# A chunked recurrence feeding routed experts: the block product moves behind u, and the fourth chunk of each group takes over work of the fifth

## Chip, cores and metric

The kernel runs on one core of a Trainium2 chip. Its engines are TensorE (PE; PEld are its weight loads), VectorE (DVE), ScalarE (ACT), GpSimd (POOL) and the queue of SyncE (SP). Each engine takes its own instructions in program order; semaphores tie them together. The metric is the device time of one execution in microseconds (us).

## What is computed

Three stages follow one another: a recurrence over 768 tokens for 4 x 8 heads of width 40, a routed layer of eight experts (320 to 1024 to 320), and a dense layer (320 to 2048 to 320, squared ReLU) on 3,072 tokens. Only the recurrence matters here:

```python
for t in range(S):
    y[:, :, t] = np.einsum('bhd,bhde->bhe', rt, state)
    Sa = np.einsum('bhde,bhe->bhd', state, at)
    state_decay = state * wt[:, :, None, :] - np.einsum('bhd,bhe->bhde', Sa, bt)
    state = state_decay + np.einsum('bhd,bhe->bhde', vt, kt)
```

The output of the recurrence chooses each token's expert (the largest of eight logits), and the tokens are scattered to their experts' slots in memory.

## The kernel before

**Chunks.** The recurrence runs over 24 chunks of 32 tokens, for all 32 heads at once. Within a chunk the dependence of tokens on each other is a triangular system: its inverse is built once per chunk, ahead of time, and the state then passes from chunk to chunk by matrix products. m is c % 4.

**The steps of chunk c**, with the tile that each writes (the letters in the traces' rows):

- `u`: new values, 64 small matmuls into pu from lu and ru, then four ScalarE copies into vu. lu is one buffer.
- `state`: 64 matmuls into ps; `state_decay`: two VectorE products into ru, which `u` of the next chunk reads. `state_t`: 16 transposes into pn, two copies into rhsY.
- `vu_t`: 16 transposes into pv, two copies into vut; `scores`: 32 matmuls into pq; `scores_mask`: two VectorE products into rq.
- `y`: 64 matmuls into py; `gate_in`: one VectorE product into xt (the chunk's output). It reads rhsY, of which there are two (c % 2), so it stands ahead of `nat_k(c + 2)`, which writes the same one.
- `nat_k`: keys, eight transposes into pk, two ScalarE copies into rhsY. `nat_n`, `nat_a`, `nat_pc`: the left side X of the block product and Pn, by transposes pa and ScalarE copies.
- `block_T`: four ScalarE copies of a chunk's inverse from TT into TB (two of them, c % 2). `solve`: the block product, 16 matmuls px from X and TB and two copies into lu.
- `load`: the chunk's E in four DMAs on ScalarE's queue. `scan`: four VectorE instructions (two scans, Pc, a reciprocal). `scale`: three products on GpSimd. `gram`: 64 matmuls into G; `gram_mask`: a ScalarE copy GM and a VectorE product N.

E is loaded nine chunks ahead, scanned and scaled nine (or eight) ahead, and its Gram products are made LA = 7 ahead.

**The inverse.** One inverse serves a group of four chunks: `inv_start` transposes GM into L and lists 27 products; each character "v" that `inv` is given makes the next one on VectorE, as a product (pr) and a reduction (into Tt or Xm). The 27th is followed by a transpose from Tt into TT. PLAN and FIRST say how many products each of the four chunks makes. A group's inverse is made during the group ahead of it.

**The gate.** `gate.xT`, `gate.logits`: transposes gpt and matmuls pl with ScalarE copies; `choose`: eight tiny VectorE instructions; `count`: eight matmuls pc, an exponential and a copy; `rank`, `rank_batch`: tiny instructions, on GpSimd until chunk 16 (`eng=G`), on VectorE after; `scatter`: a DMA issued by GpSimd. Batches are chosen and counted around every fourth chunk.

**Order.** The whole order is written out by hand (`manual_schedule`). Chunks 1 to 19 go through `chunk(c)`; chunk 0 and those from 20 on have an order of their own in `run`. PSUM tiles come from three rotating large buffers (`big`) and two small ones (`small`): the next tile in a buffer waits until the last one has been read.

Of the kernel before, what the change touches and what calls it, by code (L numbers as in the profile page):

```python
# [13 lines left out]
ALU = mybir.AluOpType  # L14
AX = mybir.AxisListType
# [20 lines left out]
class Attention:  # L36
# [478 lines left out]

    def run(self, extra, weights):
        LA, SHIFT = 7, 20
        PLAN, FIRST = (11, 9, 5, 2), (11, 9, 5, 2)
        V, G = self.nc.vector, self.nc.gpsimd
        gate = self.gate  # L520

        def fill(c, i):
            if 1 <= c <= 2:
                extra(5 * c + i, 5 * c + i + 1)
            elif 5 <= c < 14 and i == 2:
                extra(10 + c, 11 + c if c < 13 else None)

        def wload(i):
            r = (self.L, self.Tt)[i % 2].rearrange("p a b -> p (a b)")
            weights.load(i, r[:, 0:704], 1)  # L530
# [57 lines left out]
        def chunk(c):  # L588

            m, bt = c % 4, gate.batch(c)  # L590
            plan = FIRST if c < 4 else PLAN
            early, nxt = bt if c < 17 else None, gate.batch(c + 1) if c < 16 else None
            self.u(c)
            if bt and 17 <= c:
                gate.choose(*bt)
            self.y(c - 1)
            self.nat_k(c + 1)
            self.load_r(c + 1)
            self.load(c + LA + 2, 3)
            fill(c, 0)  # L600
            self.gram(c + LA)
            self.gram_mask(c + LA, True)
            if m != 3:
                self.block_T(c + 1)
            self.state(c)
            self.state_decay(c)
            self.vu_t(c)
            if m == 3:
                self.block_T(c + 1)
            self.load(c + LA + 2, 0)  # L610
            fill(c, 1)
            self.gate_in(c - 1)
            if m == 3 or c == 1:
                self.scan(c + LA + 1)
                self.scale(c + LA + 1)
            self.scores(c)
            self.scores_mask(c)
            if m == 0:
                self.inv_start(c // 4 + 1, lambda k, h: G)
                gate.invert()  # L620
            self.solve(c + 1)
            if early:
                gate.count(*early)
            self.load_v(c + 2)
            self.store_x(c - 1)
            self.load_w(c + LA + 4)
            self.load(c + LA + 2, 1)
            fill(c, 2)
            gate.xT(c - 1)
            if bt and 17 <= c:  # L630
                gate.count(*bt)
            self.nat_n(c + 2)
            self.nat_a(c + 2)
            self.nat_pc(c + 2)
            self.state_t(c + 1)
            self.load(c + LA + 2, 2)
            fill(c, 3)
            gate.logits(c - 1)
            if m != 3:
                self.inv("v" * plan[m])  # L640
            if nxt:
                gate.choose(*nxt)
            if m == 2:
                self.inv("v" * plan[3])
            if bt:
                gate.rank(*bt, eng=G if early else None)
                gate.rank_batch(*bt, eng=G if early else None)
            gate.scatter(1)
            if m != 2:
                self.scan(c + LA + 2)  # L650
                self.scale(c + LA + 2)
            fill(c, 4)
            if c == 19:
                wload(0)
                wload(1)
# [5 lines left out]
        for c in range(NC - 1):  # L661
            if 1 <= c < SHIFT:
                chunk(c)
                continue
            m = c % 4
# [64 lines left out]
            self.nat_a(c + 2)  # L730
            self.nat_pc(c + 2)
            if c == 0:
                self.inv("v" * FIRST[0])
            if c >= 21:
                self.gate_in(c, x22 if c == 22 else None)
# [20 lines left out]
        c = NC - 1  # L756
# [43 lines left out]
class Gate:  # L800
# [76 lines left out]
    def choose(self, c0, c1):  # L877
        V = self.nc.vector
        k = c1 - c0
        L = self.lg[:, c0:c1]  # L880

        def t(shape, nm):
            return self.wp.tile(shape, F32, tag=nm + str(k), name=f"{nm}_{c0}", bufs=2 if k == 1 and nm == "ex" else 1)

        def bc(z):
            return z.unsqueeze(2).to_broadcast([128, k, 8])

        mx, d, ex, eq, m2 = t([128, k], "mx"), t([128, k, 8], "d"), t([128, k, 8], "ex"), t([128, k, 8], "eq"), t([128, k], "m2")
        self.ex[c0] = ex
        V.tensor_reduce(mx, L, axis=AX.X, op=ALU.max)  # L890
        V.tensor_tensor(d, L, bc(mx), ALU.subtract)
        self.d[c0] = d
        V.tensor_scalar(eq, d, 0.0, None, ALU.is_equal)
        V.tensor_tensor(eq, eq, self.we.unsqueeze(1).to_broadcast([128, k, 8]), ALU.mult)
        V.tensor_reduce(m2, eq, axis=AX.X, op=ALU.max)
        V.tensor_tensor(self.oh[:, c0:c1], eq, bc(m2), ALU.is_equal)
        V.tensor_tensor(eq, self.oh[:, c0:c1], self.ie.unsqueeze(1).to_broadcast([128, k, 8]), ALU.mult)
        V.tensor_reduce(self.ei[:, c0:c1], eq, axis=AX.X, op=ALU.add)

    def count(self, c0, c1):  # L900

# [9 lines left out]
    def ahead(self, c0, c1, i, car, r, V):  # L911

        k = c1 - c0
        pr = self.pr[c0]
        ab, q = (self.wp.tile([128, k, 8], F32, tag=f"{nm}{i}{k}", name=f"{nm}{i}_{c0}") for nm in ("ab", "rq"))
        V.tensor_copy(ab[:, 0], car)
        for j in range(1, k):
            V.tensor_tensor(ab[:, j], ab[:, j - 1], pr[:, 2 * i + 1, j - 1], ALU.add)
        V.tensor_tensor(car, ab[:, k - 1], pr[:, 2 * i + 1, k - 1], ALU.add)
        V.tensor_tensor(ab, ab, pr[:, 2 * i], ALU.add)  # L920
        V.tensor_tensor(q, ab, self.oh[:, c0:c1], ALU.mult)
        self.sum8(V, r, q)

    def sum8(self, eng, out, q):

        if eng is self.nc.vector:
            eng.tensor_reduce(out, q, axis=AX.X, op=ALU.add)
            return
        eng.tensor_tensor(q[:, :, 0:4], q[:, :, 0:4], q[:, :, 4:8], ALU.add)
        eng.tensor_tensor(q[:, :, 0:2], q[:, :, 0:2], q[:, :, 2:4], ALU.add)  # L930
        eng.tensor_tensor(out, q[:, :, 0], q[:, :, 1], ALU.add)

    def invert(self):

# [25 lines left out]
    def rank_batch(self, c0, c1, eng=None):  # L960
        V, k = eng or self.nc.vector, c1 - c0
        sm = self.wp.tile([128, k], F32, tag=f"sm{k}", name=f"sm_{c0}")
        self.ahead(c0, c1, 1, self.cntb, self.lp[:, c0:c1], V)
        self.sum8(V, sm, self.ex.pop(c0))
        V.tensor_scalar_add(sm, sm, 1e-9)
        self.sums.append((c0, c1, sm))
        if eng is None:
            self.invert()
# [732 lines left out]
```

## Time and profile before

| | |
|---|---|
| median of 3 runs | 1104.91 us (1104.29 to 1106.89) |
| profiled execution | 1107.82 us, span of its trace 1106.0 us |
| busy, share of the span | PE 85%, PEld 76%, DVE 68%, ACT 51%, POOL 28% |
| granted TensorE clock, mean | 0.909 |
| DMA | 122.71 MB, mean 111 GB/s |
| start of `u` of chunks 1, 4, 8, 12, 16, 20 | 88.32, 144.93, 213.76, 283.02, 352.12, 415.14 us |

The span reaches from the first to the last instruction of one profiled execution. A row of the timeline gives start, length, engine, line, operation, tile written and tiles read, shapes (partitions x elements), and in brackets the idle time of the engine before it with what ended it; rows of one kind are merged. "issue" is idle time for which the trace shows no cause. PEclk is the granted clock as a share of 2.4 GHz.

### The profile page before, as it was taken

What the parts mean: (1) busy time and instruction counts of PE and PEld (TensorE: products, weight loads), DVE (VectorE), ACT (ScalarE), POOL (GpSimd) and SP (SyncE); (2) the same over time, 40 slices, a digit from 0 to 9 for tenths busy, and PEclk for the clock granted to TensorE, in tenths of its full rate; (3) what the DMA queues carried; (4) which work ended last, traced back from release to release, by engine and by line L of the source; (5) the groups of instructions that cost most, each with busy time, mean ns of one, the idle gap of its engine ahead of it and who ended that gap; (6) DMA issues with size and microseconds to landing.
All of it is one profiled execution on the core that took longest, in us unless ns stands there. A gap on an engine that the chain in (4) does not pass through costs nothing.

```text
span 1106.0 us, 30639 instructions
## 1 busy us (share of the span) xinstructions
PE 937.6 (85%) x12526; PEld 843.9 (76%) x12526; DVE 757.0 (68%) x1515; ACT 568.1 (51%) x1302; POOL 304.8 (28%) x432
## 2 busy tenths in 40 slices
PE   5257677777887878899899998799999999999995
PEld 3147676766776767768889998789899999999995
DVE  7999979799696784566887878867544444444432
ACT  7135575565665657635456655556534343434432
POOL 5523162341633110114555555414301010000000
PEclk7567889697897988889999999999999999999998
DMA  7735644364551324146766766434100000000000
GB/s 189 197 99 166 195 135 143 113 181 124 157 137 47 94 69 125 41 133 178 231 221 205 218 217 203 143 101 124 48 24 25 25 25 24 1 25 1 23 2 27
DMA packets 80647, 122.71 MB, mean 111 GB/s; under 512 B 9679, under 2 KB 57409, under 8 KB 79561
## 3 DMA queue, kind: packets, MB, share of 16 engines
q1 hardware_dynamic: 71173, 100.09, 30.5%
q10 hardware_dynamic: 7020, 12.78, 4.0%
q0 software_dynamic: 2304, 7.78, 2.2%
q8 instruction: 101, 1.65, 0.6%
q14 instruction: 49, 0.40, 0.1%
HBM read 91.36 MB, written 29.35 MB: 109 GB/s over the span
## 4 chain that ended last, share of the span: by engine, by line
PE 52%; DVE 28%; issue 6%; DMA 6%; ACT 4%; POOL 2%; SPq 1%; ACTq 0%; DVEq 0%; POOLq 0%
PE phg L1364 16%; DVE pr L268 5%; PE phe L1364 5%; PE pog L1390 5%; PE pog L1389 5%; PE pog L1388 5%; DMA xs<-zs_s 2%; DVE Tt L272 2%; PE px L388 2%; DVE ru L432 2%; DVE e L163 2%; PE poe L1390 2%; DVE wB L157 2%; PE poe L1388 2%; PE poe L1389 2%
## 5 line engine op out<-in xcount | busy, mean ns | idle before, releaser
L1374 DVE SCALAR_TENSOR_TENSOR sqg<-phg,rg 128x512 f32<-128x512 f32 x96 | 66.3, 691 | 119.0 <-ACT rg L1373 115.5
L1373 ACT ACTIVATE rg<-phg 128x512 f32<-128x512 f32 x96 | 57.3, 596 | 110.4 <-PE phg L1364 110.2
L1376 DVE TENSOR_TENSOR hlg<-sqg,hhg 128x512 fp32r<-128x512 f32 x96 | 66.6, 693 | 65.9 <-ACT hhg L1375 60.4
L388 PE MATMUL px<-TB,X 128*104 128x128 f32 x384 | 65.1, 339 | 41.9 <-ACT TB L316 34.8
L1375 ACT CAST hhg<-sqg 128x512 fp32r<-128x512 f32 x96 | 59.6, 620 | 78.6 <-DVE sqg L1374 75.4
L1364 PE MATMUL phg<-xhg,e 128*128 128x512 f32 x264 | 93.1, 393 | 0.0
L388 PEld LDWEIGHTS px<-TB,X 128*104 128x104 f32 x384 | 58.8, 220 | 44.7 <-ACT TB L316 35.8
L178 POOL TENSOR_TENSOR e<-e 104x512 f32<-104x512 f32 x21 | 28.1, 1338 | 176.4 <-PE px L388 54.9
L391 ACT COPY lu<-px 104x512 f32<-104x512 f32 x48 | 25.8, 589 | 99.1 <-PE px L388 95.9
L1390 PE MATMUL pog<-e,hlg 128*128 128x320 f32 x240 | 74.1, 309 | 0.0
L1389 PE MATMUL pog<-e,hhg 128*128 128x320 f32 x240 | 74.1, 309 | 0.0
L1388 PE MATMUL pog<-e,hhg 128*128 128x320 f32 x240 | 74.0, 308 | 0.0
L192 PE MATMUL G<-e 64*32 64x64 f32 (+1 forms) x1536 | 26.4, 254 | 46.6 <-issue 26.1
L178 POOL TENSOR_TENSOR e<-e,wB 104x512 f32<-104x512 f32 x42 | 57.3, 1382 | 23.1 <-DVE wB L157 20.0
L192 PEld LDWEIGHTS G<-e 40*32 40x32 f32 (+1 forms) x1536 | 19.5, 121 | 56.1 <-issue 29.6
L1182 POOL TENSOR_TENSOR e<-rw,e 128x256 fp32r<-128x256 f32 x51 | 43.1, 849 | 68.2 <-ACT e L1181 57.1
L470 PE MATMUL pq<-rq,vut 128*64 128x64 f32 x768 | 38.2, 243 | 23.9 <-ACT vut L461 21.2
L1364 PE MATMUL phe<-xhe,e 128*128 128x480 f32 (+4 forms) x176 | 57.9, 370 | 0.0
L316 ACT COPY TB<-TT 32x256 f32<-32x256 f32 x94 | 37.8, 402 | 39.0 <-DVE TT L307 36.6
L1364 PEld LDWEIGHTS phg<-xhg,e 128*128 128x128 f32 x264 | 49.6, 188 | 8.8
L1503 POOL DMA_INDIRECT x2g<-zs_s,idx x24 | 23.7, 989 | 113.5 <-ACT hhg L1375 105.7
L470 PEld LDWEIGHTS pq<-rq,vut 128*64 128x64 f32 x768 | 31.6, 152 | 30.6 <-ACT vut L461 27.0
(336 smaller groups left out, 2965.7 us busy)
## 6 DMA issues: line engine op xcount, KB each, us to landing
e<-in_E_dram ACTq DMA_DIRECT2D x60, 208.0 KB
rw<-in_w_dram SPq DMA_DIRECT2D x30, 320.0 KB
zs_s<-zt SPq DMA_DIRECT2D x24, 320.0 KB
rw<-in_w_dram SPq DMA_DIRECT2D x30, 256.0 KB
e<-in_E_dram SPq DMA_DIRECT2D x9, 832.0 KB
ru<-in_VR_dram SPq DMA_DIRECT2D x48, 128.0 KB
cr<-in_wi_dram SPq DMA_DIRECT2D x20, 256.0 KB
cr<-in_wo_dram SPq DMA_DIRECT2D x20, 256.0 KB
```

Source lines behind the costliest of these rows:

```text
L178: eng.tensor_tensor(z, z, f, ALU.mult)
L268: eng.tensor_tensor(pv, in0, in1, ALU.mult)
L388: self.nc.tensor.matmul(px[0:104, par, 128 * o : 128 * o + 128], X[:, par, o, :], TB[:, 4 * par + o, :], start=True, stop=True)
L470: T.matmul(pq[s, 64 * q : 64 * q + 64], vut[:, q, s], rt[:, :, q, pp], start=True, stop=True)
L1364: T.matmul(o, lt, rt, start=(i == 0), stop=(i == len(seq) - 1))
L1373: A.activation(r[:, :n], o, AF.Relu)
L1374: V.scalar_tensor_tensor(sq[:, :n], o, 0.0, r[:, :n], ALU.max, ALU.mult)
L1375: A.copy(hh[:, :n], sq[:, :n])
L1376: V.tensor_tensor(hl[:, :n], sq[:, :n], b32(hh)[:, :n], ALU.subtract)
L1388: T.matmul(o, hh[:, t], W["h2"], start=(f == 0), stop=False)
L1389: T.matmul(o, hh[:, t], W["l2"], start=False, stop=False)
L1390: T.matmul(o, hl[:, t], W["h2"], start=False, stop=(f == NF - 1))
```

## The change

Three things are changed in the order of `chunk`, and one is rewritten with the same result.

- The block product `solve(c + 1)` stands right behind `u(c)` in the chunks with m = 0, 1 and 2. The copies that it needs (`block_T`) are made a chunk earlier. In chunks with m = 3 it stands at the end.
- At the end of a chunk with m = 3, ahead of that block product, stand y, keys (`nat_k`) and Gram products that belonged to the next chunk, and both `block_T`. The chunk with m = 0 has none of these. Behind the block product the next inverse is started with its first seven products.
- Each chunk scans and scales one E (m = 3 did two, m = 2 none), and `choose` stands behind that scan. `count` stands later, and part 3 of the load stands behind the state's decay. The 27 products are split anew: 7 at the end of m = 3, 2 ahead of the scores in m = 0, and PLAN.
- `over8` takes the place of `sum8` and of the reductions in `choose`: on VectorE one reduction, on GpSimd three additions, into another tile than the input.

```diff
@@ -515,7 +515,7 @@
 
     def run(self, extra, weights):
         LA, SHIFT = 7, 20
-        PLAN, FIRST = (11, 9, 5, 2), (11, 9, 5, 2)
+        FIRST, PLAN, LAST = (11, 8, 7, 1), (6, 6, 5, 1), (6, 6, 6, 0)
         V, G = self.nc.vector, self.nc.gpsimd
         gate = self.gate
 
@@ -588,39 +588,42 @@
         def chunk(c):
 
             m, bt = c % 4, gate.batch(c)
-            plan = FIRST if c < 4 else PLAN
+            plan = FIRST if c < 4 else PLAN if c < 16 else LAST
             early, nxt = bt if c < 17 else None, gate.batch(c + 1) if c < 16 else None
+            ahead, done = m == 3 and c < 19, m == 0
             self.u(c)
+            if m != 3:
+                self.solve(c + 1)
             if bt and 17 <= c:
                 gate.choose(*bt)
-            self.y(c - 1)
-            self.nat_k(c + 1)
+            if not done:
+                self.y(c - 1)
+                self.nat_k(c + 1)
+                self.gram(c + LA)
+                self.gram_mask(c + LA, True)
             self.load_r(c + 1)
-            self.load(c + LA + 2, 3)
             fill(c, 0)
-            self.gram(c + LA)
-            self.gram_mask(c + LA, True)
-            if m != 3:
-                self.block_T(c + 1)
             self.state(c)
             self.state_decay(c)
+            self.load(c + LA + 2, 3)
             self.vu_t(c)
-            if m == 3:
-                self.block_T(c + 1)
-            self.load(c + LA + 2, 0)
+            if m < 2 or c == 19:
+                self.block_T(c + (2 if m < 2 else 1))
             fill(c, 1)
             self.gate_in(c - 1)
-            if m == 3 or c == 1:
+            if c == 1:
                 self.scan(c + LA + 1)
                 self.scale(c + LA + 1)
+            if done:
+                self.inv("v" * 2)
+                gate.invert()
             self.scores(c)
             self.scores_mask(c)
-            if m == 0:
-                self.inv_start(c // 4 + 1, lambda k, h: G)
-                gate.invert()
-            self.solve(c + 1)
-            if early:
-                gate.count(*early)
+            self.load(c + LA + 2, 0)
+            if m == 3:
+                self.inv("v" * plan[3])
+            if c == 19:
+                self.solve(c + 1)
             self.load_v(c + 2)
             self.store_x(c - 1)
             self.load_w(c + LA + 4)
@@ -636,19 +639,29 @@
             self.load(c + LA + 2, 2)
             fill(c, 3)
             gate.logits(c - 1)
+            if early:
+                gate.count(*early)
             if m != 3:
                 self.inv("v" * plan[m])
-            if nxt:
-                gate.choose(*nxt)
-            if m == 2:
-                self.inv("v" * plan[3])
             if bt:
                 gate.rank(*bt, eng=G if early else None)
                 gate.rank_batch(*bt, eng=G if early else None)
             gate.scatter(1)
-            if m != 2:
-                self.scan(c + LA + 2)
-                self.scale(c + LA + 2)
+            if ahead:
+                self.y(c)
+                self.block_T(c + 1)
+                self.nat_k(c + 2)
+            self.scan(c + LA + 2)
+            self.scale(c + LA + 2)
+            if nxt:
+                gate.choose(*nxt)
+            if ahead:
+                self.gram(c + LA + 1)
+                self.gram_mask(c + LA + 1, True)
+                self.block_T(c + 2)
+                self.solve(c + 1)
+                self.inv_start(c // 4 + 2, lambda k, h: G)
+                self.inv("v" * 7)
             fill(c, 4)
             if c == 19:
                 wload(0)
@@ -730,6 +743,7 @@
             self.nat_a(c + 2)
             self.nat_pc(c + 2)
             if c == 0:
+                self.block_T(2)
                 self.inv("v" * FIRST[0])
             if c >= 21:
                 self.gate_in(c, x22 if c == 22 else None)
@@ -887,15 +901,15 @@
 
         mx, d, ex, eq, m2 = t([128, k], "mx"), t([128, k, 8], "d"), t([128, k, 8], "ex"), t([128, k, 8], "eq"), t([128, k], "m2")
         self.ex[c0] = ex
-        V.tensor_reduce(mx, L, axis=AX.X, op=ALU.max)
+        self.over8(V, mx, L, d, ALU.max)
         V.tensor_tensor(d, L, bc(mx), ALU.subtract)
         self.d[c0] = d
         V.tensor_scalar(eq, d, 0.0, None, ALU.is_equal)
         V.tensor_tensor(eq, eq, self.we.unsqueeze(1).to_broadcast([128, k, 8]), ALU.mult)
-        V.tensor_reduce(m2, eq, axis=AX.X, op=ALU.max)
+        self.over8(V, m2, eq, ex, ALU.max)
         V.tensor_tensor(self.oh[:, c0:c1], eq, bc(m2), ALU.is_equal)
         V.tensor_tensor(eq, self.oh[:, c0:c1], self.ie.unsqueeze(1).to_broadcast([128, k, 8]), ALU.mult)
-        V.tensor_reduce(self.ei[:, c0:c1], eq, axis=AX.X, op=ALU.add)
+        self.over8(V, self.ei[:, c0:c1], eq, ex, ALU.add)
 
     def count(self, c0, c1):
 
@@ -919,16 +933,16 @@
         V.tensor_tensor(car, ab[:, k - 1], pr[:, 2 * i + 1, k - 1], ALU.add)
         V.tensor_tensor(ab, ab, pr[:, 2 * i], ALU.add)
         V.tensor_tensor(q, ab, self.oh[:, c0:c1], ALU.mult)
-        self.sum8(V, r, q)
-
-    def sum8(self, eng, out, q):
+        self.over8(V, r, q, ab, ALU.add)
+
+    def over8(self, eng, out, q, t, op):
 
         if eng is self.nc.vector:
-            eng.tensor_reduce(out, q, axis=AX.X, op=ALU.add)
-            return
-        eng.tensor_tensor(q[:, :, 0:4], q[:, :, 0:4], q[:, :, 4:8], ALU.add)
-        eng.tensor_tensor(q[:, :, 0:2], q[:, :, 0:2], q[:, :, 2:4], ALU.add)
-        eng.tensor_tensor(out, q[:, :, 0], q[:, :, 1], ALU.add)
+            eng.tensor_reduce(out, q, axis=AX.X, op=op)
+            return
+        eng.tensor_tensor(t[:, :, 0:4], q[:, :, 0:4], q[:, :, 4:8], op)
+        eng.tensor_tensor(t[:, :, 4:6], t[:, :, 0:2], t[:, :, 2:4], op)
+        eng.tensor_tensor(out, t[:, :, 4], t[:, :, 5], op)
 
     def invert(self):
 
@@ -961,7 +975,7 @@
         V, k = eng or self.nc.vector, c1 - c0
         sm = self.wp.tile([128, k], F32, tag=f"sm{k}", name=f"sm_{c0}")
         self.ahead(c0, c1, 1, self.cntb, self.lp[:, c0:c1], V)
-        self.sum8(V, sm, self.ex.pop(c0))
+        self.over8(V, sm, self.ex.pop(c0), self.d.pop(c0), ALU.add)
         V.tensor_scalar_add(sm, sm, 1e-9)
         self.sums.append((c0, c1, sm))
         if eng is None:
```

## Rows read from the trace of the kernel before

**Rows 1.** Windows: stretch, length, busy us of PE, PEld, DVE, ACT, POOL; PEclk, DMA.

```profile
135.39:341.87 206.48, 156.72 (x4573) 140.66 (x4572) 176.69 (x316) 126.09 (x307) 79.12 (x129) 0.84 0.47 138
341.87:420.50 78.63, 63.08 (x1611) 56.49 (x1613) 55.76 (x124) 50.15 (x123) 16.81 (x39) 0.83 0.26 78
```

**Rows 2.** Waits of DVE, 135.39 to 341.87: total us, times, longest.

```profile
DVE N L209 <- ACT GM L206: 16.3, 3, 6.1
DVE rq L478 <- PE pq L470: 4.0, 3, 1.9
```

**Rows 3.** Waits of DVE, 341.87 to 420.50.

```profile
DVE N L209 <- ACT GM L206: 9.1, 1, 9.1
DVE rq L478 <- PE pq L470: 4.1, 2, 2.6
```

**Rows 4.** Timeline of DVE, chunks 11 and 12.

```profile
269.32 0.59 DVE L268 TENSOR_TENSOR pr<-Xm,Tt 128x256 f32<-128x256 f32 x1
...
270.40 1.99 DVE L307 STREAM_TRANSPOSE TT<-Tt 128x1024 f32<-128x1024 f32 x1
...
279.15 1.22 DVE L157 TENSOR_TENSOR_SCAN wB<-wB,onesB 104x512 f32<-104x512 f32 x1
...
281.80 1.95 DVE L163 TENSOR_TENSOR_SCAN e<-e,zR 104x512 f32<-104x512 f32 x1
289.34 0.43 DVE L209 TENSOR_TENSOR N<-G,mN 128x256 f32<-128x256 f32 x1 [5.59 <-ACT GM L206]
```

**Rows 5.** Timeline of PE, end of chunk 11.

```profile
274.13 3.74 PE L388 MATMUL px<-TB,X 128*104 128x128 f32 x16 [2.85 <-ACT TB L316]
277.66 1.75 PE L907 MATMUL pc<-oh,mats 128*128 128x32 f32 x8
```

**Rows 6.** Windows, columns as in rows 1.

```profile
274.13:286.30 12.17, 12.17 (x211) 11.67 (x211) 9.34 (x12) 6.42 (x18) 7.61 (x13) 0.51 0.32 91
```

**Rows 7.** Timeline of PE, chunks 13 and 14.

```profile
309.55 2.00 PE L388 MATMUL px<-TB,X 128*104 128x128 f32 x16
...
313.14 0.49 PE L869 MATMUL pl<-wg,gxT 128*32 128x8 f32 x24
313.56 0.80 PE L402 MATMUL pu<-ru,lu 128*32 128x40 f32 x64
...
315.88 0.41 PE L192 MATMUL G<-e 64*32 64x64 f32 x20
317.98 0.68 PE L192 MATMUL G<-e 64*32 64x64 f32 x44 [1.69 <-issue]
318.59 1.43 PE L421 MATMUL ps<-vu,rhsY 128*40 128x40 f32 x64
```

**Rows 8.** Timeline of DVE, chunks 12 to 14.

```profile
295.08 2.16 DVE L217 STREAM_TRANSPOSE L<-GM 128x1024 f32<-128x1024 f32 x1
...
301.13 0.43 DVE L268 TENSOR_TENSOR pr<-L,Tt 128x256 f32<-128x256 f32 x1
...
302.96 0.29 DVE L268 TENSOR_TENSOR pr<-L,Tt 128x128 f32<-128x128 f32 x1
...
304.13 1.21 DVE L157 TENSOR_TENSOR_SCAN wB<-wB,onesB 104x512 f32<-104x512 f32 x1
...
307.15 0.42 DVE L209 TENSOR_TENSOR N<-G,mN 128x256 f32<-128x256 f32 x1
...
311.08 0.61 DVE L268 TENSOR_TENSOR pr<-Xm,Tt 128x256 f32<-128x256 f32 x1
...
314.77 0.69 DVE L268 TENSOR_TENSOR pr<-L,Tt 128x512 f32<-128x512 f32 x1
...
321.08 1.22 DVE L157 TENSOR_TENSOR_SCAN wB<-wB,onesB 104x512 f32<-104x512 f32 x1
```

**Rows 9.** Timeline of ACT, chunk 9.

```profile
232.35 1.59 ACT L377 ACTIVATE rhsY<-pk,sgn 64x640 f32<-64x640 f32 x2
...
234.93 1.64 ACT L316 COPY TB<-TT 32x256 f32<-32x256 f32 x4
```

## Prediction

> **What bounds the kernel now.** I read the page first: VectorE and TensorE are both near full in the recurrence over chunks of 32 tokens, and TensorE alone carries the expert layers behind it. The change touches only chunks 1 to 19, so I then measured VectorE's period: from the start of the state decay of chunk 3 to that of chunk 15 (three groups of four chunks), and from there to chunk 20 [rows 1]. Three groups take 206.48 us, 68.83 each; VectorE's busy time is 176.69 of that, and the rest is short gaps between its instructions and a few long waits. The view of waits names them [rows 2]: 16.3 us on the Gram mask N, 4.0 us on the scores' mask. That is 6.8 us a group, so 62.1 us of a group is VectorE at work with its short gaps. VectorE sets the pace; TensorE is busy 156.72 of 206.48 us and waits for it.
>
> The long wait sits once a group, behind the fourth chunk (m = c % 4 = 3). There the inverse ends (product 27, then the transpose into TT) [rows 4]; ScalarE copies TT into TB, TensorE runs px = X x TB, and only then come the transposes, u, y, pk, G, GM and N. VectorE meanwhile finishes two scans and has nothing: 5.59 us before N [rows 4]. TensorE's granted clock is 0.51, the lower level (1.2 GHz), over 274.13 to 286.30, though it is busy the whole time [rows 6]; px takes 3.74 us there [rows 5] and 2.00 us at the full clock [rows 7]. It had waited 2.85 us just before.
>
> **The change, part by part.** Instructions are the same in kind and number: 16 matmuls and 2 copies for a solve, 4 copies for block_T, 64 matmuls for y and for gram, 8 and 2 copies for nat_k, 27 products. `over8` replaces `sum8` and the reductions: on VectorE one reduction as before, on GpSimd three small additions as before into another tile; nothing. What moves is order, so I price waits.
>
> *VectorE's order.* L's transpose and products 1 to 7, 6.05 us (295.08 to 301.13 [rows 8]), go from the start of m = 0 to the end of m = 3, into the hole. The double scan of m = 3 becomes one in m = 2 and one in m = 3. Its second scan ran beside GpSimd's scale and took 4.60 us from 279.15 to the end of e [rows 4], against 3.02 from 304.13 to 307.15 [rows 8]: 1.6 us of contention leaves. Work per group becomes 62.1 - 1.6 = 60.5 us. Four new waits come on top.
>
> *m = 3 to m = 0 (the block product last).* Count from the decay's start. Decay, output, score mask 3.5 us (307.15 to 311.08 less N), product 27 1.1, TT 2.0: 6.7. ScalarE: TB 1.64 [rows 9] to 8.3, keys 1.59 [rows 9] to 9.9, GM and N to 10.7; VectorE has its scan (3.0) until 9.7 and waits 1.0 at most; transpose and products to 16.8. On ScalarE the second TB ends at 11.9, lu at 13.1; u, px for the next chunk and ps (0.8, 2.0, 1.4 [rows 7]) end at 17.3. VectorE's work in this stretch is 16.1, so about 1.1 us of wait: the lower bound. The upper bound is the lower clock. TensorE has less to do before this point than now (the block product was taken away), so it waits longer for VectorE and the clock is likely down when the tail starts, 2.2 us in. At full clock the tail from gpt to pk without u is 3.6 us (px's end at 311.55 to G at 315.88 [rows 7], less 0.7 for u); at px's ratio of 1.87 it is 6.8; pc 1.75 [rows 5]; G 1.1 plus a stall as the 1.69 us of rows 7; px 3.74, less 0.9 because the low stretch lasted 12.2 us [rows 6]: 16.4. With lu 0.6, u 0.8, px 2.0 and ps 1.4 the decay comes at 21.2: 5.1 us of wait. I take 3.5, a little above the middle, because the wait in front makes the low clock the likelier state.
>
> *m = 0.* y, keys and Gram product are gone from it; products 8 and 9 cover the score mask's wait. Behind the mask VectorE has products 10 to 15 (1.17 + 3.69 [rows 8]), a scan 3.0 and N 0.4: 8.3 us of cover. TensorE needs pl, u, y, pk (313.14 to 315.88, 2.74), px 2.00, G 1.05 without its stall and ps 1.43 [rows 7]: 7.2, or 8.9 with a stall. I take 0.3; bounds 0 and 0.6. This is also where the solve is queued ahead: behind it on TensorE wait y, keys, Gram and state product, and for those VectorE's decay.
>
> *m = 1.* Products 16 to 20 alone are 6.31 us (314.77 to 321.08 [rows 8]), so cover is 9.7; no wait at the decay. The score mask follows decay and output closely and waits for vut and pq, as it does now in 4.0 us over three groups [rows 2]: 0.7, bounds 0 and 0.9.
>
> *m = 2.* The scan now stands in front of `choose`, whose eight tiny instructions run while GpSimd scales. The second scan lost 1.6 us in such company; if that fell on two of its four instructions, each lost 0.8 (an estimate), and the three instructions of a scale can catch three: bounds 0 and 2.4. I take 0.9, about one caught; this is a choice. The GPSIMD Engine Reference of the Trainium skill (1. Specifications) says that GpSimd shares its SBUF interface with VectorE and collides with instructions with two SBUF inputs; `choose` has four such, and by that rule alone the cost would be the upper 2.4 and the time 5 us longer. Rows 4 agree that the collision exists; its count is open.
>
> Group: 60.5 + 3.5 + 0.3 + 0.7 + 0.9 = 65.9 us, 2.9 less than 68.83; three groups 8.8.
>
> *Chunks 15 to 20.* 78.63 us [rows 1], 13.2 of them waits [rows 3]; 65.4 stay. One scan (3.0) leaves, product 27 and TT (3.1) enter: 65.5. New waits: at chunk 15 no scan covers, 3.5 + 3.0; at chunk 16 cover is only products 10 to 15, 4.9, against 6.2 (7.2 without G): 1.3; chunk 17 0.7. Together 74.0: 4.6 less. Bounds 7.7 less and 2.8 less. block_T(20) no longer waits for TT; that is inside.
>
> *Chunks 0 to 3.* VectorE loses product 27 and TT and gains a scan: even. The solve in chunk 1 comes at a low clock and choose gets a scan beside it: 1 us more, bounds 0 and 2.5.
>
> *Queues.* Part 3 of the load is issued behind the decay in place of ahead of the Gram product; its reader, the scan, is still a chunk's work away. On GpSimd the ranks of m = 3 now stand before the only scale of that chunk; its reader is the Gram product two chunks on. SP's loads of r wait for y: y of m = 3 comes earlier, so none is later. Nothing of these is on the path; if part 3 landed late the scan would wait for it directly.
>
> Sum: 8.8 + 4.6 - 1.0 = 12.4 us. The profiled execution took 1107.8 us; against it 1095.4. The median of the runs is 2.9 lower, 1104.9, so I forecast 1092.
>
> **The rivals.** *VectorE without a hole.* If the clock stays up, all lower bounds hold: a group 61.6 (21.7 for three), 7.7 and 0: 29 us, 1076. For it: the dense runs of small matmuls, where G stalls [rows 7], are broken up by the solve in m = 0 to 2. Against it: rows 6.
>
> *The hole only moves.* Upper bounds: a group at 69.5 (2.0 more for three), chunks 15 to 20 at 75.8 (2.8 less), the start 2.5 more: 2 us slower than now, 1107; with one of the bounds not reached, 1105, no change. For it: the low clock at m = 3 now comes with 2.9 us of wait in front, and the new order waits longer there. TensorE: Matmul & The Clock Gate of the Trainium skill (Loop structure matters more than you think) says that a wait between bursts of matmuls leaves the clock low for the next burst. Rows 5 and 6 agree, and by that rule alone this rival would be the forecast, at 1105.
>
> *The block product in front of the state product.* Slower. In m = 0 and 1 the solve stands between u and the state product. If those starts run at the lower level, 7.2 becomes 13.5 at px's ratio: 5.2 of wait in m = 0 and 3.8 in m = 1, 5.3 more at chunk 16, against the forecast 31 us in all over the seven places. It decides from about half of that (16 us: 1108); with two thirds, 1113. For it: cover in m = 0 is 1.1 us above the chain. Against it: before these starts TensorE has u, px, ps, pv and pq nearly in a row, and the clock recovered in rows 6 after 12 us of such work.
>
> **How the numbers follow.** Forecast 0.55 (1084 to 1100), no hole 0.17, the hole moves 0.16, slower 0.12. Leaving out the slower case and half of the no-hole case (0.2 in all) gives 1077 to 1107. A difference under 0.3% (3.3 us) can't be told from none. Faster 0.72, same 0.16, slower 0.12.
>
> **What would show it.** Right: groups of about 66 us between the decays of chunks 3, 7, 11, 15; the 16.3 us on N falls under 9; products 1 to 7 directly behind the Gram mask of m = 3; a scan in every chunk at 3.0 us; px of m = 0 to 2 at 2.0 us. Wrong: px at 3.7 us in those chunks with VectorE waiting for ps (third rival); VectorE waiting over 4 us for N or ps after m = 3 (second); two-input instructions of choose at 1 us. The forecast fails high if the clock is low in the starts of m = 0, and low if TensorE's stalls at G vanish.

## The result and the profile after

The changed kernel takes 1116.31 us (median of 7 runs, 1110.93 to 1120.68), the kernel before in the same session 1104.83 us (7 runs). The ratio is 1.0101, with a 95% interval of 1.0072 to 1.0130: 1% slower, outside the predicted range of 1077 to 1107 and on the wrong side. The profiled execution after has a span of 1114.5 us, 8.5 us more than before, and a mean granted clock of 0.894. All ratios are of fast runs; one run of those below was slow and is left out of its ratio, the traced one of y1_scatter_behind (1121.10 us), though its median has it.

I divide both traces at the starts of the state decay, as in [rows 1]. "Before chunk 0" is the start of the first decay itself.

| stretch | before, us | after, us | difference | forecast |
|---|---|---|---|---|
| before chunk 0 | 75.19 | 77.48 | +2.3 | 0 |
| chunks 0 to 3 | 60.20 | 64.37 | +4.2 | +1.0 |
| chunks 3 to 15 (three groups) | 206.48 | 216.80 | +10.3 | -8.8 |
| chunks 15 to 20 | 78.65 | 71.95 | -6.7 | -4.6 |

What remains up to the span, -1.6 us, lies behind chunk 20, nearly all of it behind the decay of chunk 22. The loss sits in the three groups, so they come first. These are the windows of the kernel after, with the columns of rows 1:

```profile
141.85:358.65 216.80, 166.69 (x4572) 148.43 (x4572) 191.83 (x316) 127.82 (x306) 75.07 (x129) 0.78 0.45 129
358.65:430.60 71.95, 58.83 (x1611) 52.54 (x1613) 55.78 (x124) 50.66 (x123) 12.87 (x35) 0.85 0.26 80
```

VectorE executes 316 instructions in the first window, as many as before, but is busy 191.83 us where [rows 1] have 176.69: 15.1 us more "work" with the same work to do. The waits of VectorE in that window, which answer to rows 2, went down by 3.6 us in sum:

```profile
DVE N L209 <- ACT GM L206: 13.2, 6, 3.3
DVE rq L478 <- PE pq L470: 3.5, 5, 1.1
```

So the waits did what they were forecast to do, roughly, and single instructions became longer. The timeline of the kernel after shows two places. The first is the end of chunk 10 (a third chunk, m = 2), VectorE and GpSimd side by side:

```profile
281.33 0.19 DVE L905 TENSOR_TENSOR d<-lg,mx 128x32 f32<-128x32 f32 x1
281.37 1.28 POOL L178 TENSOR_TENSOR e<-e 104x512 f32<-104x512 f32 x1 [10.18 <-PE pv L458]
281.56 1.13 DVE L907 TENSOR_SCALAR eq<-d 128x32 f32<-128x32 f32 x1
282.61 2.48 POOL L178 TENSOR_TENSOR e<-e,wB 104x512 f32<-104x512 f32 x2
282.72 1.21 DVE L908 TENSOR_TENSOR eq<-eq,we 128x32 f32<-128x32 f32 x1
283.96 0.19 DVE L941 TENSOR_REDUCE m<-eq 128x4 f32<-128x32 f32 x1
284.18 0.96 DVE L910 TENSOR_TENSOR oh<-eq,m 128x32 f32<-128x32 f32 x1
285.17 0.19 DVE L911 TENSOR_TENSOR eq<-oh,ie 128x32 f32<-128x32 f32 x1
```

These are tiny instructions of `choose` on 32 elements a partition. Free of GpSimd one takes 0.19 us; beside each of the three products of the scale (the row ending in `x2` holds two of them) one takes 1.0 to 1.2. That is 2.7 us lost. The second place is the end of chunk 11 (m = 3), where the inverse's products 6 and 7 now run:

```profile
303.56 0.31 DVE L268 TENSOR_TENSOR pr<-L,Tt 128x144 f32<-128x144 f32 x1
303.65 1.16 POOL L987 DMA_INDIRECT zs_s<-xt,sli  x1 [0.50 <-DVE Tt L272]
303.90 0.30 DVE L272 TENSOR_REDUCE Tt<-pr 128x24 f32<-128x144 f32 x1
304.24 4.55 DVE L268 TENSOR_TENSOR pr<-L,Tt 128x196 f32<-128x196 f32 x1
304.84 1.28 POOL L178 TENSOR_TENSOR e<-e 104x512 f32<-104x512 f32 x1
306.08 2.48 POOL L178 TENSOR_TENSOR e<-e,wB 104x512 f32<-104x512 f32 x2
308.82 0.36 DVE L272 TENSOR_REDUCE Tt<-pr 128x28 f32<-128x196 f32 x1
309.10 1.65 DVE L432 TENSOR_TENSOR ru<-ps,Pc 40x640 f32<-40x640 f32 x2
```

Product 7 takes 4.55 us, until GpSimd's scale is over. Its neighbours in size, products 6 and 8, take 0.31 us here and 0.43 in [rows 8]; with no scale beside it product 7 takes 0.36 (x2, below), so 4.2 us are lost. The state decay behind it (`ru`) starts at 309.10, although TensorE's state product (`ps` in the next fence) was complete at 306.68. The same hold of 4.5 to 4.6 us is there at chunk 7, and at chunk 3 on product 5. At chunk 15, which has no scale, it isn't.

TensorE's end of the fourth chunk is the other candidate. Its timeline in the kernel after, with the window that answers to rows 6:

```profile
288.18 0.90 PE L867 MATMUL gpt<-ident,xt 128*128 128x128 f32 x3 [4.47 <-DVE xt L501]
291.96 1.91 PE L921 MATMUL pc<-oh,mats 128*128 128x32 f32 x8
297.73 3.74 PE L388 MATMUL px<-TB,X 128*104 128x128 f32 x16
305.25 1.43 PE L421 MATMUL ps<-vu,rhsY 128*40 128x40 f32 x64
```

```profile
288.18:301.06 12.88, 12.88 (x211) 11.89 (x211) 9.41 (x11) 8.75 (x23) 5.24 (x21) 0.50 0.32 98
```

Behind a wait of 4.47 us the whole tail runs at the lower of TensorE's two levels (1.2 GHz, granted 0.50), `px` takes 3.74 us as in [rows 5], and VectorE waits 3.2 us for `N`. So two theories went to the chip. **Shared access:** VectorE's instructions are held while GpSimd's products run, and this is the loss. **Clock:** the low tail is the loss, and the hold is slack, since the decay would have waited for TensorE anyway.

### The profile page after: what moved, and what is told of

Same layout as the page of the kernel before. It is cut to its first block, busy times and chain, and to the rows that moved or that the text cites. A ratio compares the mean times of both kernels' runs of the same rounds, so it can differ in the third digit from the quotient of the medians.

```text
span 1114.5 us, 30611 instructions
## 1 busy us (share of the span) xinstructions
PE 943.4 (85%) x12526; PEld 849.0 (76%) x12526; DVE 775.4 (70%) x1515; ACT 570.8 (51%) x1302; POOL 300.1 (27%) x432
## 4 chain that ended last, share of the span: by engine, by line
PE 52%; DVE 26%; DMA 6%; issue 5%; ACT 5%; SPq 2%; POOL 2%; ACTq 0%; DVEq 0%; POOLq 0%
PE phg L1378 16%; DVE pr L268 5%; PE pog L1404 5%; PE pog L1403 5%; PE pog L1402 5%; PE px L388 3%; PE phe L1378 3%; DVE ru L432 2%; DMA xs<-zs_s 2%; DMA e<-in_E_dram 2%; DVE Tt L272 2%; DVE pr L300 1%; DVE rq L478 1%; PE pk L344 1%; DVE e L163 1%
## 5 line engine op out<-in xcount | busy, mean ns | idle before, releaser
L1388 DVE SCALAR_TENSOR_TENSOR sqg<-phg,rg 128x512 f32<-128x512 f32 x96 | 66.3, 690 | 119.0 <-ACT rg L1387 119.0
L1390 DVE TENSOR_TENSOR hlg<-sqg,hhg 128x512 fp32r<-128x512 f32 x96 | 66.5, 693 | 65.9 <-ACT hhg L1389 63.2
L178 POOL TENSOR_TENSOR e<-e,wB 104x512 f32<-104x512 f32 x42 | 54.0, 1305 | 25.1 <-DVE wB L157 17.8
L1404 PE MATMUL poe<-e,hle 128*120 128x320 f32 (+4 forms) x150 | 47.6, 318 | 5.9 <-DVE hle L1383 5.9
L1378 PE MATMUL phg<-xlg,e 128*128 128x512 f32 x132 | 51.7, 392 | 0.0
L867 PE MATMUL gpt<-ident,xt 128*128 128x128 f32 (+1 forms) x66 | 15.9, 364 | 40.8 <-DVE xt L501 40.8
```

The source lines that it names most:

```text
L178: eng.tensor_tensor(z, z, f, ALU.mult)
L1378: T.matmul(o, lt, rt, start=(i == 0), stop=(i == len(seq) - 1))
L1388: V.scalar_tensor_tensor(sq[:, :n], o, 0.0, r[:, :n], ALU.max, ALU.mult)
L1390: V.tensor_tensor(hl[:, :n], sq[:, :n], b32(hh)[:, :n], ALU.subtract)
L1404: T.matmul(o, hl[:, t], W["h2"], start=False, stop=(f == NF - 1))
```

## The experiments

Each is compared with runs of the kernel before on the same chip. Times in us are medians; I go by the ratio to the kernel before, as the medians of the kernel before differ by up to 2.6 us between sessions. A difference to the changed kernel is worked out from two such ratios.

| label | edit | median | ratio to before, 95% interval |
|---|---|---|---|
| (changed kernel) | | 1116.31 | 1.0101 (1.0072 to 1.0130) |
| x1_choose_first | `choose` ahead of scan and scale | 1102.27 | 0.9966 (0.9937 to 0.9996) |
| x2_scale_before_ranks | scale ahead of the ranks | 1105.79 | 0.9990 (0.9950 to 1.0029) |
| x3_both | both moves | 1093.86 | 0.9893 (0.9859 to 0.9926) |
| x4_no_scale | scale left out, m = 2 and 3 | 1089.51 | 0.9878 (0.9820 to 0.9936) |
| y1_scatter_behind | indirect DMA behind the scale | 1109.27 | 1.0020 (0.9992 to 1.0048) |
| y2_both_solve_late | x3, block product late | 1094.18 | 0.9883 (0.9856 to 0.9911) |
| y3_both_warm | x3, 14 more matmuls | 1104.50 | 0.9979 (0.9948 to 1.0010) |
| y4_warm_alone | changed kernel, 14 more matmuls | 1126.14 | 1.0172 (1.0136 to 1.0207) |
| z1_both_warm6 | x3, 6 more matmuls | 1100.12 | 0.9927 (0.9895 to 0.9958) |
| z2_both_warm3 | x3, 3 more matmuls | 1094.99 | 0.9882 (0.9849 to 0.9916) |
| z3_before_scan_clear | kernel before, first scale later in the text | 1104.84 | 0.9981 (0.9952 to 1.0010) |

**`choose` out of the scale's way.** The scale waits for its own scan, so a `choose` that VectorE runs ahead of the scan is over before GpSimd starts.

```diff
-            self.scan(c + LA + 2)
-            self.scale(c + LA + 2)
             if nxt:
                 gate.choose(*nxt)
+            self.scan(c + LA + 2)
+            self.scale(c + LA + 2)
```

> In the chunks that are third of four (c2, c6, c10, c14) the router's `choose` on VectorE is issued ahead of the scan and of GpSimd's scale of `e`, not behind them. Shared-access theory (VectorE's instructions on data in SBUF are held while GpSimd's products run): the three instructions of `choose` that took 1.13, 1.21 and 0.96 us return to about 0.2 each, 2.7 us less in each of four chunks, in sum some -10.8: about 1105.5 us, 1103 to 1109. Clock theory (what the changed kernel lost, it lost by the low level of TensorE's clock behind the block product of the fourth chunks): nothing changes, 1115 to 1118.

1.3% less than the changed kernel, 14.9 us and a little more than expected; the kernel is level with the one before again or a little faster. In its timeline the three instructions have their short times back, at the end of the same chunk:

```profile
269.47 0.18 DVE L907 TENSOR_SCALAR eq<-d 128x32 f32<-128x32 f32 x1
269.69 0.19 DVE L908 TENSOR_TENSOR eq<-eq,we 128x32 f32<-128x32 f32 x1
...
270.13 0.19 DVE L910 TENSOR_TENSOR oh<-eq,m 128x32 f32<-128x32 f32 x1
```

The held product is still there, 4.54 to 4.55 us at chunks 3, 7 and 11. The three groups take 207.75 us (-9.1, three times 2.7 and a little), and chunks 0 to 3 take 59.85 (-4.5; of these 2.7 are `choose`, and the rest is a wait in chunk 1 that comes and goes between runs, see below).

**The scale ahead of the ranks.** GpSimd works through its queue in order; in the fourth chunks of the changed kernel the ranks and the scatter stood in front of the scale and carried it onto the products.

```diff
-            if bt:
-                gate.rank(*bt, eng=G if early else None)
-                gate.rank_batch(*bt, eng=G if early else None)
-            gate.scatter(1)
+            if bt and not early:
+                gate.rank(*bt)
+                gate.rank_batch(*bt)
+            if not (bt and early):
+                gate.scatter(1)
...
             self.scale(c + LA + 2)
+            if bt and early:
+                gate.rank(*bt, eng=G)
+                gate.rank_batch(*bt, eng=G)
+                gate.scatter(1)
```

> In the fourth chunks GpSimd's scale of `e` is issued ahead of the router's ranks and scatter, so it should be done before VectorE reaches the inverse's products. Shared-access theory: the product that took 4.5 us (the 128x196 one at c7 and c11, the 128x100 one at c3) takes 0.36 again, and the next state decay starts 2.4 to 3.5 us sooner, three times: about -9, some 1107 us, 1104 to 1111. Clock theory: the state product of the next chunk comes when it did, the held product was slack, 1115 to 1118.

1.1% less than the changed kernel, some 12 us. In the timeline the scale now lies in VectorE's wait for `N` and ends as the transpose of L begins; product 7 takes 0.36 us, and the decay of chunk 12 waits for TensorE instead:

```profile
285.89 1.27 POOL L178 TENSOR_TENSOR e<-e 104x512 f32<-104x512 f32 x1 [10.54 <-PE py L492]
287.12 2.49 POOL L178 TENSOR_TENSOR e<-e,wB 104x512 f32<-104x512 f32 x2
...
294.50 0.36 DVE L268 TENSOR_TENSOR pr<-L,Tt 128x196 f32<-128x196 f32 x1
...
296.00 1.66 DVE L432 TENSOR_TENSOR ru<-ps,Pc 40x640 f32<-40x640 f32 x2 [0.75 <-PE ps L421]
```

The steps from a fourth chunk to the next first one go from 23.2, 23.2 and 23.1 us to 19.6, 19.7 and 19.8: about 3.5 of the 4.2 us of each hold were on the path.

**Both moves.** The two diffs above together.

> Both moves at once: `choose` ahead of the scan and scale in the third chunks, the scale ahead of the ranks in the fourth. Shared-access theory: the two gains add, about -20, some 1096 us, 1092 to 1101, under both kernels. Clock theory: 1115 to 1118.

2.1% less than the changed kernel, 23 us, and 1.07% less than the kernel before: this version beats both. The windows and waits of its three groups:

```profile
137.33:336.14 198.81, 156.13 (x4572) 138.09 (x4572) 171.46 (x316) 127.44 (x306) 72.13 (x130) 0.85 0.48 141
```

```profile
DVE N L209 <- ACT GM L206: 9.3, 3, 3.3
DVE rq L478 <- PE pq L470: 5.1, 4, 2.4
DVE ru L432 <- PE ps L421: 4.6, 4, 1.7
```

VectorE's busy time falls by 20.4 us against the changed kernel, for the same 316 instructions, and ends 5.2 under the kernel before. A group takes 66.3 us; the prediction had 65.9. Against the kernel before the three groups take 7.7 us less, and most of it is not the filled hole: 5.2 is busy time, near the 4.8 that the prediction gave to the second scan's contention, while the waits on `N`, `rq` and `ru` only go from 21.3 us (16.3, 4.0 and 1.0) to 19.0.

**No scale.** The move could hide another cause, so the scale was taken away where it stands.

```diff
-            self.scale(c + LA + 2)
+            if m < 2:
+                self.scale(c + LA + 2)
```

> Leaves out part of the computation: GpSimd's scale of `e` in the chunks that are third and fourth of four, with everything else in its place. Shared-access theory: both holds go, as in the kernel with both moves, about 1096 us, 1091 to 1101. Clock theory: GpSimd is off the path, 1115 to 1118. If the two moves give less than this one, the scale costs VectorE something wherever it stands.

2.2% less than the changed kernel, about as much as both moves; the median lies 1.5 us under the expected range. Its three groups take 195.03 us, 3.8 less than with both moves: by these two traces the scale still costs about 1.3 us a group where it stands there. The clock theory expected no change from any of these four; as the cause of the loss it is refuted. The clock moved, though: over the three groups the granted share is 0.84 before, 0.78 in the changed kernel and 0.85 with both moves, so a lower clock came with the holds and left with them.

**The indirect DMA in front of the scale.** Product 7 had begun 0.6 us before the first product of the scale, while GpSimd issued the scatter's indirect DMA.

```diff
-            gate.scatter(1)
+            if not (bt and early):
+                gate.scatter(1)
...
             self.scale(c + LA + 2)
+            if bt and early:
+                gate.scatter(1)
```

> The changed kernel with one thing moved: in the fourth chunks the scatter, which GpSimd issues between the ranks and the scale, is issued behind the scale. The held product began while that indirect DMA was being issued, so either it or the three products of the scale could be what holds. If the products of the scale do it: the scale starts about 1.2 us sooner, an earlier product of VectorE's inverse is caught and held some 4 us, until the scale ends, and the next state decay comes 1 to 2 us sooner, three times: 1110 to 1114 us. If the issue of the indirect DMA does it: no product takes over 1 us in the fourth chunks, and the gain is that of the scale ahead of the ranks, about 1106.

0.8% less than the changed kernel, about 9 us, and neither case in its pure form. With the scatter behind the scale no instruction is held through the whole scale; a GpSimd product holds one instruction at most, as in `choose`. At chunk 11, two are held:

```profile
299.06 1.27 POOL L178 TENSOR_TENSOR e<-e 104x512 f32<-104x512 f32 x1
299.10 0.26 DVE L272 TENSOR_REDUCE Tt<-pr 128x20 f32<-128x100 f32 x1
299.39 1.10 DVE L268 TENSOR_TENSOR pr<-L,Tt 128x144 f32<-128x144 f32 x1
300.28 2.69 POOL L178 TENSOR_TENSOR e<-e,wB 104x512 f32<-104x512 f32 x2
300.53 0.30 DVE L272 TENSOR_REDUCE Tt<-pr 128x24 f32<-128x144 f32 x1
300.87 0.98 DVE L268 TENSOR_TENSOR pr<-L,Tt 128x196 f32<-128x196 f32 x1
```

The loss there is 1.4 us (1.10 and 0.98 against 0.31 and 0.36), and 2.3 at chunk 3, where three products are caught. This is the only trace of this order, and of its longest execution (1121.10 us), so I read from it what is held and for how long, and no more. The kernel without the scale has the other half. There the indirect DMA is issued beside the products as in the changed kernel, with no scale behind it, and product 7 of chunk 11, begun in the middle of it, takes its usual time:

```profile
283.53 1.06 POOL L988 DMA_INDIRECT zs_s<-xt,sli  x1 [0.51 <-issue]
284.24 0.37 DVE L268 TENSOR_TENSOR pr<-L,Tt 128x196 f32<-128x196 f32 x1
```

So the products of the scale hold VectorE, and the indirect DMA alone does not; where it stood right in front of the products, the loss was two to three times as long. Why is open: in those places the held instruction had also begun before the first product of the scale, and in the others after one.

**The block product late again.** In the kernel with both moves the headline of the change is undone for m = 0 to 2: the solve goes back behind the scores.

```diff
             self.u(c)
-            if m != 3:
-                self.solve(c + 1)
...
-            if c == 19:
+            if m != 3 or c == 19:
                 self.solve(c + 1)
```

> The kernel with both moves (1093.9 us), and the block product of the first three of four chunks put back behind the scores, as in the kernel before. If the early block product is what gains: the waits on `N` come back in these chunks, 16.3 us over twelve chunks of the kernel before or 1.4 a chunk, over some 14 chunks +15 to +19: 1106 to 1113 us. If it earns nothing and the gain is from the second scan that no longer runs beside the scale: 1092 to 1097.

The same as with both moves (0.9883 and 0.9893). Its three groups take 196.66 us, and its waits on `N` are 9.1 us in three places, all behind the fourth chunks. So in the kernel without the holds the place of the block product in these chunks neither gains nor costs. My +15 to +19 was also badly worked out: I spread the 16.3 us on `N` over twelve chunks, though [rows 2] say that there are three, one a group.

**More matmuls for the clock.** 14 matmuls of a constant follow the scores in the fourth chunks, with both moves and alone.

```diff
             self.state(c)
+            psw = self.st["ps", c]
...
+            if ahead:
+                for i in range(14):
+                    self.nc.tensor.matmul(psw[:, i % 2, 384:512], idle[:, 0:128], idle[:, 0:128], start=True, stop=True)
             self.load(c + LA + 2, 0)
```

> The kernel with both moves, and 14 matmuls of a constant into a free part of the state product's bank behind the scores of each fourth chunk, so that TensorE isn't idle before the long tail. Clock theory, now with the holds gone: the tail runs at the upper level, the wait on `N` of 2.8 to 3.3 us goes, `px` takes 2.0 and not 2.8: -3 to -3.5 in each of four chunks, about 1081, 1078 to 1085. If the tail's length isn't set by the clock: 1092 to 1097.

> The changed kernel with those 14 matmuls alone, and the scale where it was. Clock theory: -4.5 in each of three groups, about 1102. Shared-access theory: the held product ends with GpSimd's scale, whose start hangs on the ranks and not on TensorE, so the state decay comes when it did; what gain there is comes at c15, which has no scale: 1113 to 1117.

Both are slower than without the matmuls, by about 0.9% and 0.7%, which no theory expected. TensorE's timeline in the first shows why:

```profile
273.89 5.98 PE L625 MATMUL ps<-mats 128*128 128x128 f32 x28 [0.67 <-DVE ru L432]
279.71 0.49 PE L876 MATMUL gpt<-ident,xt 128*128 128x128 f32 x3
...
281.88 1.08 PE L930 MATMUL pc<-oh,mats 128*128 128x32 f32 x8
...
285.88 2.00 PE L388 MATMUL px<-TB,X 128*104 128x128 f32 x16
```

I had put them into the state product's bank, so they wait for the decay, and then they last 5.98 us. The tail behind them does run at the upper level (`pc` 1.08 and not 1.91, `px` 2.00 and not 3.74), but it starts later by more than that saves: at chunk 11 `gpt` starts 7.5 us after the decay of that chunk, and 2.2 after it in the changed kernel.

Fewer matmuls, 6 or 3, into the bank that `vut` was copied from, with both moves:

```diff
-        pv = self.big(f"pv{c}")
+        pv = self.pv = self.big(f"pv{c}")
...
+            if ahead:
+                for i in range(6):
+                    self.nc.tensor.matmul(self.pv[:, i % 2, 0:128], idle[:, 0:128], idle[:, 0:128], start=True, stop=True)
```

> The kernel with both moves, and 6 matmuls of a constant behind the scores of each fourth chunk, now into the bank from which `vut` was copied, so that they need not wait for the state decay as the 14 did. At the 0.43 us that one of those took they need 2.6 us, which lies in the 3.2 us that TensorE idles there. Clock theory: with the hole filled the tail runs at the upper level (`pc` 1.08 and not 1.91, `px` 2.0 and not 2.8), the wait on `N` of 3 us goes, -3 in each of four chunks: about 1082, 1079 to 1086. If so few matmuls do not raise the clock: 1092 to 1097, with `pc` at 1.9.

> The same with 3 matmuls, 1.3 us of the 3.2 us hole. Clock theory: part of the gain at most, 1086 to 1094; otherwise 1092 to 1097.

No gain: 0.9927 and 0.9882 against 0.9893; with 6 the time, 1100.12 us, is above both expected ranges. With 6, one of the three tails has `pc` at the upper level and little wait for `N`; the two others have `pc` at 1.91, and waits of 3.0 and 2.5 us. VectorE's and TensorE's rows of the one, at chunk 11:

```profile
274.80 1.08 PE L929 MATMUL pc<-oh,mats 128*128 128x32 f32 x8
...
280.83 0.42 DVE L209 TENSOR_TENSOR N<-G,mN 128x256 f32<-128x256 f32 x1 [0.89 <-ACT GM L206]
```

With both moves alone that wait is 2.80 us, and the step from chunk 11 to 12 takes 19.4 us against 17.4 here. So the low level does set the wait for `N`, by 2 us in that group, but filling the hole in this way didn't pay.

**The kernel before without the contention of its second scan.**

```diff
             if m == 3 or c == 1:
                 self.scan(c + LA + 1)
+            if c == 1:
                 self.scale(c + LA + 1)
             self.scores(c)
             self.scores_mask(c)
+            if m == 3:
+                self.scan(c + LA + 2)
+                self.scale(c + LA + 1)
...
+            if m < 2:
+                self.scan(c + LA + 2)
             if m != 2:
-                self.scan(c + LA + 2)
                 self.scale(c + LA + 2)
```

> The kernel before, with one thing moved: in the fourth chunks the first of the two scales is issued behind both scans, so that the second scan, which took 4.6 us beside it and not 3.0, runs alone. If the contention was on the path: -1.6 in each of four chunks, 1098 to 1101. If the wait on `N` behind it (5.6 us) takes up what is freed: 1103 to 1107, and the wait on `N` grows to about 7.

VectorE's order stayed as it was and GpSimd's too, so neither theory was tested: the time is the same and so is the contention.

```profile
281.48 1.26 POOL L178 TENSOR_TENSOR e<-e 104x512 f32<-104x512 f32 x1 [17.87 <-PE px L388]
...
282.70 3.47 POOL L178 TENSOR_TENSOR e<-e,wB 104x512 f32<-104x512 f32 x2
283.91 1.08 DVE L160 TENSOR_TENSOR Pc<-wB,e 104x16 f32<-104x16 f32 x1
...
285.31 1.94 DVE L163 TENSOR_TENSOR_SCAN e<-e,zR 104x512 f32<-104x512 f32 x1
```

GpSimd has its own queue, and its scale still starts right behind the first scan. Where the line stands among VectorE's lines is nothing to it.

## Why the prediction was wrong

**The step that failed** is "products 1 to 7, 6.05 us, go into the hole", together with, under *Queues*, "On GpSimd the ranks of m = 3 now stand before the only scale of that chunk; its reader is the Gram product two chunks on" and "Nothing of these is on the path". I asked who reads the scale's result, and not what VectorE executes while the scale runs. Before, the scale of that place ran beside the scores' mask, which takes 1.39 us there and 1.36 to 1.39 elsewhere, and the transpose of L, which takes 2.16 us there [rows 8] and 2.06 in the kernel after: no loss worth the name. GpSimd's rows before, chunk 12:

```profile
293.27 1.29 POOL L178 TENSOR_TENSOR e<-e 104x512 f32<-104x512 f32 x1
294.50 2.54 POOL L178 TENSOR_TENSOR e<-e,wB 104x512 f32<-104x512 f32 x2
```

The change moved the transpose and products forward and pushed the scale back behind the ranks, and so put products under it. A price of 6.05 us read in one place was carried to another where it is 10.1 (299.10 to 309.18). x2 shows it: with the scale elsewhere, product 7 is back at 0.36 us and the step about 3.5 us shorter.

**The term that was mis-sized** is `choose` beside the scale: the mechanism was named, 0.9 us was taken (bounds 0 and 2.4), and 2.7 is measured, above the upper bound. I priced a caught instruction at 0.8 us from a scan's; a caught one loses 0.8 to 1.0, and the three GpSimd products catch one each. My condition "two-input instructions of choose at 1 us" is met, though one of the three has a single input. x1 shows its size by itself: the three instructions lose 2.7 us in each of the four chunks of the changed kernel, and nothing in x1.

**The other terms:**

- Waits behind m = 3: 3.5 predicted, 3.2 on `N` measured in the changed kernel; with both moves another 0.7 to 1.7 on the state product comes to light, 4.5 in the mean, within the bounds.
- m = 0: 0.3 (to 0.6) predicted; VectorE waits 1.40, 1.33 and 0.74 us for `N` there. Mis-sized. The `px` in this place, between the decays of m = 0 and m = 1, takes 3.5 to 3.6 us, and 2.8 to 3.7 in x1 and y4, which keep the hold in front of it; in x2 and x3, without the hold, it takes 1.99 in all three groups, and the wait is gone. So the wait goes with the hold, but not with it alone: z1, without it, has such a `px` and a wait of 1.39 us in one of its three groups.
- m = 1: 0.7 predicted, 0.57, 0.70 and 0.88 measured.
- The second scan's contention left, as predicted: `e`'s scan takes 1.23 us in the mean over twelve.
- Sum of a group: 65.9 + 1.8 (`choose`) + 4.2 (held product) + 0.9 (m = 0) - 0.3 (m = 3) = 72.5; measured 216.80 / 3 = 72.3. The forecast's sum comes out where the collisions are taken out, 66.3 in x3, but in part by luck: there the waits behind m = 3 and on the scores' mask are 1.0 us above their terms each, `choose` costs nothing where 0.9 stood, and the work is 0.6 less.
- Chunks 15 to 20: 4.6 less predicted, 6.7 measured, inside its bounds. Chunks 0 to 3: +1.0 predicted, +4.2 measured, above the bound of 2.5. `choose` in chunk 2 is 2.7 of it: the step from chunk 2 to 3 takes 21.3 us, and 18.7 in x1 and x3. The other part is what the prediction had named, the block product of chunk 1 at a low clock: `px` takes 3.66 us there (granted 0.53), and VectorE waits 1.74 for `N`. In x1, x4, y3 and z2 the same `px` takes 1.99 us and that wait isn't there; in x2, x3, y1, y4 and z1 it takes 3.3 to 3.7 and the wait is 1.5 to 2.6 us. Why it differs between runs is open.
- The 2.3 us before chunk 0 aren't explained: other kernels with the same start have that decay at 74.5 to 77.7 us.

**The rivals.** "The block product in front of the state product" gave nearly the right time, 1113, by luck. Half of its sign is there: `px` of m = 0 runs near the lower level in the changed kernel, and not in x3 (TensorE between the decays of chunks 12 and 13, first the changed kernel, then x3):

```profile
315.62 3.62 PE L388 MATMUL px<-TB,X 128*104 128x128 f32 x16
```

```profile
295.40 1.99 PE L388 MATMUL px<-TB,X 128*104 128x128 f32 x16
```

But VectorE waits for `ps` nowhere in the three groups, and its waits for `N` in m = 0 are 3.5 us in all. In the kernel without the holds, y2 moves the block product back and nothing changes; in the changed kernel itself that was not run. "The hole only moves" describes the tail rightly (granted 0.50, `px` 3.74), but its price is not the loss: x3 keeps that tail at chunks 3 and 7 (granted 0.50) and part of it at chunk 11 (0.64), and is 1% faster than before.

The page "SBUF — State Buffer" of the Trainium skill (SBUF: two separate sides) says that VectorE and GpSimd share a pair of ports by an exclusive lock, which the one that starts first holds for the whole instruction while the other is blocked, and it counts as VectorE's side the instructions with two SBUF inputs (against a GpSimd instruction that reads SBUF) and those in a two-port mode. The rows agree on who is held, in that tiny instructions take 1.0 to 1.2 us beside a product of 1.25, and reductions and the transpose aren't; a hold of one instruction over three products, 4.55 us, is more than that rule gives. Taking the upper bound for `choose`, as by that rule alone, would have given 5 us of the 24 that were missed: the rule had to be asked of every place where the scale would land.

## What to carry to other kernels

When instructions of VectorE are moved, or GpSimd's queue is reordered, lay the two timelines over each other in the new order and ask what VectorE executes during each large GpSimd instruction; a reader that is two chunks away says nothing about it. Put GpSimd's large two-input products beside VectorE's waits, transposes and reductions, and keep runs of short products and compares out of them: here two moves of a few lines, with no instruction added or removed, turned 1% slower into 1% faster. And when an engine's busy time grows while its instruction count stands still, look for instructions that are held, not for waits.

## What the runs showed of the hardware that was not expected

- An instruction of 0.36 us took 4.55 us, over three GpSimd products in a row, where the products followed an indirect DMA that GpSimd issued; without that DMA in front a product held one instruction at most, for 1.0 to 1.1 us (y1), and the DMA without the products held none (x4). The reason is open.
- A VectorE instruction with one tensor input (the compare L907, on 32 elements a partition) was held as the two-input ones were: 1.13 us against 0.18. Reductions beside the same products took their usual 0.19.
- Small GpSimd instructions (the ranks, 0.2 us each) beside the products of the inverse cost them nothing that the rows show: in x2 product 7 takes 0.36 us amid them.
